# Attention and two wide MLPs on one core: the preparation of the second weights paced anew

## The chip, the cores and the metric

The kernel runs on one core of one Trainium2 chip. The metric is the device time of one execution in microseconds (us), the median of several runs. The engines are named as in the profile: PE is TensorE's matmul, PEld its weight load, DVE is VectorE, ACT is ScalarE, POOL is GpSimd, SP is SyncE, whose queue issues nearly all DMAs here.

## What is computed

An attention whose keys and values are averaged over groups of 8 positions, and two MLPs over its 4608 output rows, all in float32:

```
B, H, S, D = 8, 8, 576, 64          # d_model 512, d_ff 2048
k_p, v_p = mean of k, v over 8 neighbouring positions
attn = softmax(q @ k_p^T / sqrt(D));  x = attn @ v_p       # 4608 x 512
h = x @ w_in;   g = maximum(0.01 * h, h);  x = g @ w_out   # first MLP
h = x @ w_in2;  r = maximum(h, 0);         x = (r * r) @ w_out2   # second MLP
```

The weights of both MLPs come as 64-bit floats and have to be made into 32-bit ones on the chip.

## The kernel before, in words

**Stages.** Attention and the first MLP on 2048 rows run together as four plain tiles of 512 rows (`units`, `first`, `second`). The other 2560 rows of the first MLP and all rows of the second go through nine passes t = 0 to 8 (`HALVES`): passes 0, 1 and 2 are the first MLP (2 x 384, 2 x 384 and 2 x 512 rows, `t < LEAD`), passes 3 to 8 the second MLP (2 x 384 rows each). Every pass has a first half, `first2` (rows times w_in), and a second half, `second2` (times w_out), each of 28 blocks: four slices a = 0 to 3 by seven products 1 to 7 of half matrices, in the manner of Strassen and Winograd. A block takes 12 matmuls in the passes that matter here. The order of products in a second half of passes 0 to 2 is 1, 5, 6, 2, 7, 3, 4, with a running inside.

**What a block needs.** Its weights come over SP's queue into a ring of six buffers (`next_block`, tiles `wb...`, numbered through the program: wb84 to wb111 are the second half of pass 1, wb112 on is pass 2). Products 3, 5, 6 and 7 come as plain float32; ACT rounds them to the upper part (L1118) and DVE subtracts (L1119) to get the lower part. The matmuls are three per product of parts: upper by upper, upper by lower, lower by upper. In a second half the other operand, `oh` (ACT, L1027) and `ol` (DVE, L1028), is made by `split_g` from `g`; there are four buffers of each. Beside that, the second half of pass t makes the operands of pass t + 1: chains of a difference `d` (DVE, L1031), its upper part `xh` (ACT), its lower part `xl` (DVE). Pass 2 has 512 columns, so those chains, made in pass 1's second half, are cut in two and twice as many.

**The preparation of the second weights** (`prepare_products`, L302) has nothing to do with the rows. For each of 8 pairs p and for `in` and `out` it loads two 64-bit slices (`st...`), puts the 32-bit float together (`decode`: ACT L223 absolute value, DVE L225 clamp, L228 shift, L232 join, ACT L241 and DVE L242 low bits), makes four sums (DVE L282 to L286), splits (ACT L324, DVE L325) and stores two results to DRAM. DVE has 10 instructions for an `in` block and 11 for an `out` block, 21 for a pair, 168 in all. The generator yields 7 times for `in` and 8 times for `out`, so a pair is 15 steps and the whole 120, with one more to end it.

**Who calls it.** `prepare_step` (L1363) makes one step. In the last plain tile it is called 2 times for each f below 12 and 3 times after. In the passes it is called after a block (a hook; 56 in a pass, 112 in passes 0 and 1) for three hooks of four, until 105 steps are done, and again from pass 2 on, where the staging pools are opened anew with one buffer instead of two. It has to be over when pass 3 begins.

**What sets the order on an engine.** The program's order is not the order in the queues: a scheduler lists the instructions of every engine by its own estimate of when they are ready, so a step lands earlier or later than the hook at which it is written. On the chip each of DVE and ACT works through its list in order.

Of the kernel before, what the change touches and what calls it, by code (L numbers as in the profile page):

```python
# [32 lines left out]
def attention_two_mlps(  # L33
# [21 lines left out]
    NF = DFF // P  # L55
# [10 lines left out]
    HALVES = (384, 384, 512) + (384,) * 6  # L66
    GROWN = 2
    PADS = {0: 88, GROWN: 88, 3: 48}
    PREP_AHEAD = 105
    LEAD = 3  # L70
    NPASS = len(HALVES) - LEAD
    HMAX = max(HALVES)
# [229 lines left out]
    def prepare_products():  # L302

        for p in range(NQ):
            for kind in ("in", "out"):
                st = fetch_weights(2, [(kind, p), (kind, p + NQ)])
                yield
                ops = ppool.tile([P, 4, HD], F32, tag="ops", name=f"ops_{kind}{p}")
                words = ops.bitcast(U32)
                if kind == "in":  # L310
                    words = words.rearrange("p (i a) x -> p i (a x)", i=2)
                else:
                    words = words.rearrange("p (a i) x -> p i a x", i=2)
                for _ in decode(st, words, f"{kind}2_{p}"):
                    yield
                yield
                s = raw(mpool.tile([P, 2, TT], U32, tag="m", name=f"s2_{kind}{p}"))
                s = s.rearrange("p i (a x) -> p (i a) x", a=2)
                sums(s, *(ops[:, i] for i in range(4)))
                later(1, out=WS[2, kind, p // 2][:, :, p % 2].rearrange("o p x -> p o x"), in_=s)  # L320
                yield
                hl = ppool.tile([P, 3, 2, HD], F32R, tag="hl", name=f"hl2_{kind}{p}")
                for d, i in ((slice(0, 2), slice(0, 2)), (slice(2, 3), slice(3, 4))):
                    nc.scalar.copy(hl[:, d, 0], ops[:, i])  # L324
                    nc.vector.tensor_tensor(out=hl[:, d, 1], in0=ops[:, i], in1=raw(hl[:, d, 0]), op=ALU.subtract)  # L325
                later(
                    3, out=WD[2, kind, p // 2][:, :, p % 2].rearrange("o p x -> p o x"),
                    in_=raw(hl).rearrange("p o h x -> p o (h x)"),
                )
                yield  # L330
# [658 lines left out]
    FIRST2 = []  # L989
# [362 lines left out]
    at_work, due = True, 0  # L1352
    prep, preparing, hooks, prepared = None, True, 0, 0
# [21 lines left out]
    for i, (t, f) in enumerate(units):  # L1375
        if f == NF - 3 and t + 1 < NTILE:
            while ready[0] * S < min((t + 2) * TT, PLAIN):
                advance()
            put_stores(made)
            load_x(t + 1)  # L1380
        if f == NF - 1 and t + 1 < NTILE:
            split_x(t + 1)

        rate = RATES[min(t, 1)]
        if i + 1 < len(units):
            first(*units[i + 1])
        tick()
        if i + 2 < len(units):
            split_weights("in", *units[i + 2])
        if i + 1 < len(units):  # L1390
            split_weights("out", *units[i + 1])
        while at_work and made < due + rate // 2:
            advance()
        second(t, f)
        tick()
        due += rate
        while at_work and made < due:
            advance()
        if w1 < NF:
            prepare_weights(w1)  # L1400
            w1 += 1
        elif t > 0:
            held(lambda: next(sums1, None))
        if i == NF:
            behind(marks[0], 3000)
        if t == NTILE - 1 and f >= NQ - 2 and not at_work:
            if x2pool is None:
                assert not at_work and next(sums1, 1)
                w_early_stack.close()
                x2pool = high_stack.enter_context(tc.tile_pool(name="x2", bufs=1, side="right", reuse_waits="tile"))  # L1410
                dpart = high_stack.enter_context(tc.tile_pool(name="d2", bufs=1, side="right", reuse_waits="tile"))
                ring = high_stack.enter_context(tc.tile_pool(name="ring", bufs=RING, side="right", reuse_waits="tile"))
                load_x2(0)
                tick(9)
                blocks.insert(0, next_block())
            else:
                if xg is None:
                    xg = products_x(0)
                for _ in range(2):
                    next(xg, None)  # L1420
        if x2pool is not None:
            if prep is None:
                ppool = prep_stack.enter_context(tc.tile_pool(name="prep", bufs=1, side="right", reuse_waits="tile"))
                prep = prepare_products()
            for _ in range(2 if f < NF - 4 else 3):
                prepare_step()
    for _ in xg:
        pass
# [14 lines left out]
    for t in range(LEAD + NPASS):  # L1443
# [12 lines left out]
        for half in (first2, second2):  # L1456
            for _ in half(t):
                tick()
                hooks += 1
                if hooks % 4 and (prepared < PREP_AHEAD or t >= GROWN):  # L1460
                    prepare_step()


# [27 lines left out]
```

## Time and profile before

| | us |
|---|---|
| three runs | 1634.41, 1638.08, 1639.64 |
| median | 1638.08 |
| profiled execution, its own time | 1636.4 |
| span of the profiled execution | 1634.7 |
| PE busy in it | 1596.6 |
| DVE busy in it | 1376.9 |
| ACT busy in it | 985.9 |

The passes lie in the span as follows: the last plain tile ends at 526.6 us; pass 0 runs to 645.3 us (halves from 527.6 and 587.4 us), pass 1 to 777.7 us (halves from 645.3 and 707.5 us), pass 2 to 930.3 us (halves from 777.7 and 854.1 us). The bounds are the places where PE's operands turn from `wb_in` to `wb_out` and back. "Busy" of an engine is the union of its instructions' times; the wait in brackets behind an instruction is the engine's idle time before it, with what released it.

### The profile page before, as it was taken

To read this page: it belongs to the slowest core of one execution; us is meant where nothing else is said; L and a number is where in the kernel's file an instruction comes from. 1 tells how busy PE (TensorE), PEld (TensorE's weight loads), DVE (VectorE), ACT (ScalarE), POOL (GpSimd) and SP (SyncE) were. 2 spreads that over 40 slices of the span, in tenths; PEclk is the share of its full clock that TensorE was granted. 3 is DMA by queue.
4 is the path that set the end of the run, shared out by engine and by line. 5 is a ranking of instruction groups with operands and counts; after the bars stand their busy time and mean duration, and the time that the engine had idled before them with its cause. 6 is when DMAs were issued, how large, how long until landed. Compare 5 with 4: busy or idle time off the path is not lost.

```text
span 1634.7 us, 25145 instructions
## 1 busy us (share of the span) xinstructions
PE 1596.6 (98%) x8680; PEld 1433.0 (88%) x8680; DVE 1376.9 (84%) x2049; ACT 985.9 (60%) x1845; POOL 119.3 (7%) x146
## 2 busy tenths in 40 slices
PE   6999999999999999998999999999999999999999
PEld 5877888888887999997888898998998998998997
DVE  6998778788868899899849589789799799799697
ACT  6787677655665776776556447456446455455454
POOL 3202232223210000000000000000000000000000
PEclk9999999999999999999999999999999999999999
DMA  8765536676454997997754664865865766756655
GB/s 217 230 207 152 152 100 189 202 242 211 147 172 149 318 317 262 316 323 223 261 187 124 214 215 147 287 194 150 275 192 170 259 180 195 237 180 204 203 166 176
DMA packets 225327, 340.89 MB, mean 209 GB/s; under 512 B 55728, under 2 KB 138672, under 8 KB 225200
## 3 DMA queue, kind: packets, MB, share of 16 engines
q1 hardware_dynamic: 222048, 337.58, 65.0%
q10 hardware_dynamic: 3152, 1.70, 0.4%
q8 instruction: 69, 1.13, 0.3%
q14 instruction: 58, 0.48, 0.1%
HBM read 268.44 MB, written 69.21 MB: 207 GB/s over the span
## 4 chain that ended last, share of the span: by engine, by line
PE 75%; DVE 13%; DMA 4%; ACT 4%; issue 3%; POOL 1%; SPq 0%; ACTq 0%; DVEq 0%; POOLq 0%
PE psum L1219 14%; PE psum L337 12%; PE psum L336 12%; PE psum L335 12%; PE psum L1220 7%; PE h L335 2%; PE h L337 2%; DVE ol L1028 2%; PE h L336 2%; PE acc L335 2%; PE acc L336 2%; PE acc L337 2%; PE s L611 2%; DMA wb_in<-ws_in 1%; DVE xl L1028 1%
## 5 line engine op out<-in xcount | busy, mean ns | idle before, releaser
L1219 PE MATMUL psum<-wb_out,oh 128*128 128x512 f32 x1008 | 350.6, 392 | 0.0
L335 PE MATMUL psum<-xh,wb_in 128*128 128x384 f32 (+1 forms) x1008 | 343.9, 341 | 4.1 <-DVE g L1199 1.2
L336 PE MATMUL psum<-xl,wb_in 128*128 128x384 f32 (+1 forms) x1008 | 343.2, 341 | 0.0
L337 PE MATMUL psum<-xh,wb_in 128*128 128x384 f32 (+1 forms) x1008 | 342.2, 340 | 0.6 <-DVE wb_in L1119 0.6
L1027 ACT CAST oh<-g 128x768 fp32r<-128x768 f32 (+1 forms) x252 | 216.2, 860 | 177.5 <-PE psum L1219 71.4
L1220 PE MATMUL psum<-wb_out,ol 128*128 128x256 f32 x1008 | 281.0, 280 | 0.0
L1028 DVE TENSOR_TENSOR ol<-g,oh 128x768 fp32r<-128x768 f32 (+1 forms) x252 | 246.7, 982 | 11.8 <-ACT oh L1027 11.0
L1219 PEld LDWEIGHTS psum<-wb_out,oh 128*128 128x128 f32 x1008 | 189.2, 188 | 41.8 <-issue 0.8
L335 PEld LDWEIGHTS psum<-xh,wb_in 128*128 128x128 f32 x1008 | 189.2, 188 | 11.5 <-DVE g L1199 1.9
L337 PEld LDWEIGHTS psum<-xh,wb_in 128*128 128x128 f32 x1008 | 189.1, 188 | 5.2 <-DVE wb_in L1119 0.9
L336 PEld LDWEIGHTS psum<-xl,wb_in 128*128 128x128 f32 x1008 | 189.4, 188 | 4.4
L1220 PEld LDWEIGHTS psum<-wb_out,ol 128*128 128x128 f32 x1008 | 189.3, 188 | 0.2
L1119 DVE TENSOR_TENSOR wb_in<-wb_in 128x512 fp32r<-128x512 f32 x144 | 97.8, 688 | 91.1 <-ACT wb_in L1118 91.0
L1031 DVE TENSOR_TENSOR g<-g,g 128x768 f32<-128x768 f32 (+1 forms) x144 | 140.4, 982 | 2.3 <-ACT g L1140 2.0
L1118 ACT CAST wb_in<-wb_in 128x512 fp32r<-128x512 f32 x144 | 89.0, 620 | 77.9 <-DMA wb_in<-ws_in 71.2
L337 PE MATMUL psum<-oh,wb_out 128*128 128x384 f32 (+1 forms) x336 | 118.7, 357 | 6.0 <-DVE wb_out L1119 6.0
L335 PE MATMUL psum<-oh,wb_out 128*128 128x384 f32 (+1 forms) x336 | 118.0, 354 | 1.9 <-ACT oh L1027 1.9
L336 PE MATMUL psum<-ol,wb_out 128*128 128x384 f32 (+1 forms) x336 | 119.2, 355 | 0.3 <-DVE ol L1028 0.3
L1118 ACT CAST wb_out<-wb_out 128x512 fp32r<-128x512 f32 x144 | 89.2, 619 | 41.7 <-DMA wb_out<-ws_out 41.2
L335 PE MATMUL h<-xh,hl_in 128*128 128x512 f32 x256 | 104.0, 406 | 4.3 <-ACT hl_out L260 2.4
L335 PE MATMUL acc<-gh,hl_out 128*128 128x512 f32 x256 | 103.6, 407 | 0.2
L336 PE MATMUL h<-xl,hl_in 128*128 128x512 f32 x256 | 100.7, 393 | 0.5 <-DVE xl L711 0.5
(171 smaller groups left out, 2976.5 us busy)
## 6 DMA issues: line engine op xcount, KB each, us to landing
wb_in<-wd_in SPq DMA_DIRECT2D x108, 512.0 KB, 3.8
wb_out<-wd_out SPq DMA_DIRECT2D x108, 512.0 KB, 4.3
wb_in<-ws_in SPq DMA_DIRECT2D x144, 256.0 KB, 3.2
wb_out<-ws_out SPq DMA_DIRECT2D x144, 256.0 KB, 2.7
out_dram<-o SPq DMA_DIRECT2D x23, 384.0 KB, 5.1
v<-in_v_dram SPq DMA_DIRECT2D x16, 512.0 KB, 4.6
st_in_out<-in_moe_w_in_dram SPq DMA_DIRECT2D x16, 512.0 KB, 4.0
st_in_out<-in_moe_w_out_dram SPq DMA_DIRECT2D x16, 512.0 KB, 5.0
```

The source lines that it names most:

```text
L335: nc.tensor.matmul(outp, ah, bh, start=first, stop=False, **kw)
L336: nc.tensor.matmul(outp, ah, bl, start=False, stop=False, **kw)
L337: nc.tensor.matmul(outp, al, bh, start=False, stop=last, **kw)
L611: nc.tensor.matmul(sc[:n, 2 * m:2 * m + 2].rearrange("p a x -> p (a x)"), qT[:, 2 * e + m, :n], kT[b % 2][:, 2 * e + m].rearrange("p a x - ...
L1027: nc.scalar.copy(hi, src)
L1028: nc.vector.tensor_tensor(out=lo, in0=src, in1=raw(hi), op=ALU.subtract)
L1031: nc.vector.tensor_tensor(out=out_, in0=a, in1=b, op=ALU.subtract)
L1118: nc.scalar.copy(whole[:, 0], raw(whole[:, 1]))
L1119: nc.vector.tensor_tensor(out=whole[:, 1], in0=raw(whole[:, 1]), in1=raw(whole[:, 0]), op=ALU.subtract)
L1219: nc.tensor.matmul(outp, ah, b, start=first, stop=False, skip_group_check=True)
L1220: nc.tensor.matmul(outp[:, 1], al, b[:, 0], start=False, stop=last, skip_group_check=True)
```

## The change

Three numbers of the pace are changed, and one yield is added. The last plain tile calls 3 steps for every f (30 instead of 24). In passes 0 and 1 the steps done may not exceed 30 + 0.56 for each hook, up to 90 instead of 105. From pass 2 on they may not exceed 90 + 0.75 for each hook. Blocks begun after step 90 have one empty step more behind their loads, so 35 steps are left for pass 2, four of them empty.

```diff
-    PREP_AHEAD = 105
+    PREP_AHEAD = 90
+    PACE = (30, 0.56, 0.75)
@@ prepare_products
                 st = fetch_weights(2, [(kind, p), (kind, p + NQ)])
                 yield
+                if prepared > PREP_AHEAD:
+                    yield
@@ last plain tile
-            for _ in range(2 if f < NF - 4 else 3):
+            for _ in range(3):
                 prepare_step()
@@ passes
                 tick()
                 hooks += 1
-                if hooks % 4 and (prepared < PREP_AHEAD or t >= GROWN):
+                due = PACE[0] + PACE[1] * hooks
+                if t >= GROWN:
+                    due = PREP_AHEAD + PACE[2] * (hooks - 2 * GROWN * len(FIRST2))
+                if prepared < (due if t >= GROWN else min(due, PREP_AHEAD)):
                     prepare_step()
```

No matmul, load or store is added or left out; the 168 DVE instructions of the preparation stay 168. Counted in DVE's queue, cut where the first result of a first half (`g2_t_0_11`) and the last slice's `g2_t_3_12` are read:

| stretch of DVE's queue | preparation before | now |
|---|---|---|
| up to pass 0 | 42 | 43 |
| pass 0, first half | 29 | 28 |
| pass 0, second half | 23 | 22 |
| pass 1, first half | 32 | 31 |
| pass 1, second half | 31 | 12 |
| pass 2, first half | 11 | 32 |

Of the 31 of pass 1's second half, 21 stand in DVE's queue ahead of `o2_1_3`, the last result of that half that DVE reads, and 10 behind it; now 3 ahead and 9 behind.

The first place is DVE's queue in the second half of pass 1, at the weights of product 3 (`wb103` is the last block of product 7, `wb104` the first of product 3). `ol2_1_a_k` is the lower part for slice a and product k, `xl2_2` and `d2_2` are the chains for pass 2, `wm_out2_6` is the preparation of pair 6. Before:

```order
L225 TENSOR_SCALAR wm_out2_6_8327<-wm_out2_6_8327 128x1024
L1031 TENSOR_TENSOR d2_2_7_1_0_8324<-xl2_2_7_8067,xl2_2_1_8015 128x256
L228 TENSOR_SCALAR wm_out2_6_8327<-wm_out2_6_8327 128x1024
L1028 TENSOR_TENSOR xl2_2_5_8210<-d2_2_7_1_0_8324,xh2_2_5_8211 128x256
L1119 TENSOR_TENSOR wb103_out3_7_8329<-wb103_out3_7_8329 128x512
L1031 TENSOR_TENSOR d2_2_7_1_0_8324<-xl2_2_3_8093,d2_2_7_1_0_8324 128x256
L1028 TENSOR_TENSOR ol2_1_1_3_8397<-g2_1_1_22_7502,oh2_1_1_3_8396 128x768
L1028 TENSOR_TENSOR xl2_2_6_8212<-d2_2_7_1_0_8324,xh2_2_6_8213 128x256
L232 SCALAR_TENSOR_TENSOR wm_out2_6_8327<-st2_out6_out14_8296,wm_out2_6_8327 128x1024
L1031 TENSOR_TENSOR d2_2_7_1_0_8324<-xl2_2_2_8043,d2_2_7_1_0_8324 128x256
L1119 TENSOR_TENSOR wb104_out0_3_8358<-wb104_out0_3_8358 128x512
```

Now:

```order
L1034 TENSOR_TENSOR d2_2_7_1_0_8282<-xl2_2_7_8031,xl2_2_1_7983 128x256
L1031 TENSOR_TENSOR ol2_1_3_7_8302<-g2_1_3_12_7762,oh2_1_3_7_8301 128x768
L1031 TENSOR_TENSOR xl2_2_5_8176<-d2_2_7_1_0_8282,xh2_2_5_8177 128x256
L1122 TENSOR_TENSOR wb103_out3_7_8285<-wb103_out3_7_8285 128x512
L1034 TENSOR_TENSOR d2_2_7_1_0_8282<-xl2_2_3_8054,d2_2_7_1_0_8282 128x256
L1031 TENSOR_TENSOR ol2_1_0_3_8330<-g2_1_0_22_7362,oh2_1_0_3_8329 128x768
L1031 TENSOR_TENSOR xl2_2_6_8178<-d2_2_7_1_0_8282,xh2_2_6_8179 128x256
L1122 TENSOR_TENSOR wb104_out0_3_8313<-wb104_out0_3_8313 128x512
```

Pair 6 of the preparation is gone from between the splits, and the splits of `wb103` and `wb104` stand four instructions apart.

The second place is ACT's queue at the end of the same half and the beginning of pass 2 (`oh2_1_a_4` is the last product, `wm_in2_7` the absolute value of pair 7, which needs the loaded `st2_in7`). Before:

```order
L324 CAST hl2_out6_8546<-ops_out6_8326 128x256
L223 ACTIVATE wm_in2_7_8711<-st2_in7_in15_8692 128x1024
L1027 CAST xh2_2_7_8214<-d2_2_3_0_256_8484 128x256
L1027 CAST oh2_1_1_4_8509<-g2_1_1_11_7499 128x768
L1118 CAST wb113_in0_5_8590<-wb113_in0_5_8590 128x512
```

Now:

```order
L1030 CAST oh2_1_1_4_8467<-g2_1_1_11_7478 128x768
L1030 CAST xh2_2_4_8175<-d2_2_7_1_256_8359 128x256
L1030 CAST oh2_1_2_4_8499<-g2_1_2_11_7625 128x768
L1030 CAST xh2_2_7_8180<-d2_2_3_0_0_8391 128x256
L1030 CAST oh2_1_3_4_8518<-g2_1_3_11_7761 128x768
L1121 CAST wb113_in0_5_8543<-wb113_in0_5_8543 128x512
```

No preparation stands among ACT's last operands of the half any more.

The third place is ACT's queue in the middle of that half, where now the only preparation of ACT in it stands (`so5_1` is the copy of product 5's sum, `st2_in6` the load of pair 6). Now:

```order
L1313 COPY so5_1_7925<-psum_6140 128x768
L1030 CAST xh2_2_6_8179<-d2_2_7_0_0_8181 128x256
L1030 CAST oh2_1_0_2_8126<-g2_1_0_21_7361 128x768
L224 ACTIVATE wm_in2_6_8680<-st2_in6_in14_8644 128x1024
L1030 CAST oh2_1_1_2_8149<-g2_1_1_21_7480 128x768
L1030 CAST xh2_2_4_8175<-d2_2_7_0_0_8181 128x256
L242 ACTIVATE ops_in6_8679<-st2_in6_in14_8644 128x1024
L1030 CAST oh2_1_2_2_8167<-g2_1_2_21_7627 128x768
```

Before, the absolute value of pair 6 stood between the operands of product 6 (`oh2_1_0_6` and `oh2_1_1_6`); now it stands between those of product 2. Its two loads stood around the loads of `wb91` and `wb92` in SP's queue, and stand now around that of `wb96`.

## Rows read from the trace of the kernel before

**Rows 1.** The page, busy time of the engines: us (share of the span) xinstructions.

```profile
PE 1596.6 (98%) x8680; PEld 1433.0 (88%) x8680; DVE 1376.9 (84%) x2049; ACT 985.9 (60%) x1845; POOL 119.3 (7%) x146
```

**Rows 2.** Busy time by stretch, from the last plain tile to pass 3.

```profile
core 0: us, PE busy (x) PEld busy (x) DVE busy (x) ACT busy (x) POOL busy (x), PEclk, DMA share, GB/s
472.00:526.60 54.60, 54.19 (x237) 44.00 (x235) 46.09 (x80) 38.19 (x69) 0.00 (x0) 1.00 0.59 204
527.60:587.40 59.80, 58.64 (x337) 58.32 (x338) 50.72 (x75) 40.97 (x59) 0.00 (x0) 1.00 0.93 314
587.40:645.30 57.90, 56.94 (x328) 56.41 (x327) 56.80 (x84) 42.66 (x65) 0.00 (x0) 1.00 0.85 282
645.30:707.50 62.20, 60.84 (x348) 59.93 (x348) 55.11 (x82) 43.69 (x64) 0.00 (x0) 1.00 0.91 310
707.50:777.70 70.20, 62.98 (x342) 60.06 (x341) 67.29 (x109) 47.37 (x76) 0.00 (x0) 0.98 0.81 266
777.70:854.10 76.40, 75.58 (x334) 62.23 (x333) 48.99 (x61) 44.55 (x55) 0.00 (x0) 1.00 0.69 227
854.10:930.30 76.20, 76.20 (x338) 63.12 (x337) 64.98 (x74) 43.22 (x56) 0.00 (x0) 1.00 0.51 154
930.30:988.50 58.20, 58.20 (x336) 57.92 (x335) 45.33 (x55) 28.71 (x40) 0.00 (x0) 1.00 0.70 224
```

**Rows 3.** PE's waits in pass 1's second half: us in total, times, longest.

```profile
PE psum L337 <- DVE wb_out L1119: 5.0, 4, 1.7
PE psum L335 <- ACT oh L1027: 1.9, 1, 1.9
```

**Rows 4.** Busy time and granted clock in the stretch behind these waits.

```profile
768.40:773.00 4.60, 4.60 (x17) 4.21 (x17) 4.60 (x9) 3.23 (x5) 0.00 (x0) 0.63 0.34 114
```

**Rows 5.** DVE's instructions in pass 1's second half: start, us, what [idle before].

```profile
718.10 0.69 DVE L1119 TENSOR_TENSOR wb_out<-wb_out 128x512 fp32r<-128x512 f32 x1
718.70 0.95 DVE L1031 TENSOR_TENSOR g<-g,g 128x768 f32<-128x768 f32 x1
719.57 0.95 DVE L1028 TENSOR_TENSOR ol<-g,oh 128x768 fp32r<-128x768 f32 x1
...
721.91 0.69 DVE L225 TENSOR_SCALAR wm_in<-wm_in 128x1024 f32<-128x1024 f32 x1
722.51 0.69 DVE L1119 TENSOR_TENSOR wb_out<-wb_out 128x512 fp32r<-128x512 f32 x1
...
726.93 1.22 DVE L232 SCALAR_TENSOR_TENSOR wm_in<-st_in_in,wm_in 128x1024 uint32<-128x1024 uint32 x1
728.06 1.82 DVE L1028 TENSOR_TENSOR ol<-g,oh 128x768 fp32r<-128x768 f32 x2
...
732.41 0.42 DVE L282 TENSOR_TENSOR s_in<-ops_in 128x256 f32<-128x256 f32 x1
732.74 0.42 DVE L283 TENSOR_TENSOR s_in<-ops_in 128x256 f32<-128x256 f32 x1
...
737.11 0.42 DVE L1031 TENSOR_TENSOR d<-xl,d 128x256 f32<-128x256 f32 x1
737.45 0.95 DVE L1028 TENSOR_TENSOR ol<-g,oh 128x768 fp32r<-128x768 f32 x1
...
749.13 0.69 DVE L1119 TENSOR_TENSOR wb_out<-wb_out 128x512 fp32r<-128x512 f32 x1
...
761.91 0.68 DVE L1119 TENSOR_TENSOR wb_out<-wb_out 128x512 fp32r<-128x512 f32 x1
...
767.16 0.42 DVE L1028 TENSOR_TENSOR xl<-d,xh 128x256 fp32r<-128x256 f32 x1 [1.16 <-ACT xh L1027]
```

**Rows 6.** ACT's instruction that waits at the end of that half.

```profile
765.72 1.12 ACT L223 ACTIVATE wm_in<-st_in_in 128x1024 f32<-128x1024 f32 x1 [2.58 <-DMA st_in_in<-in_moe_w_in_dram]
```

**Rows 7.** The load of the preparation in that half: KB each, median us to landing.

```profile
st_in_in<-in_moe_w_in_dram SPq DMA_DIRECT2D x4, 512.0 KB, 5.6
```

**Rows 8.** PE's one wait in pass 2's first half.

```profile
784.07 0.50 PE L335 MATMUL psum<-xh,wb_in 128*128 128x512 f32 x1 [0.82 <-ACT s L1189]
```

## The prediction

> **What bounds the kernel now.** The page's first part comes first: PE is busy 1596.6 us of a span of 1634.7 [rows 1], so not more than 38.1 us can be won by anything that leaves the matmuls as they are. Where those lie is read from the busy time by stretch [rows 2]. From the second half of pass 2 on PE is busy all the time (76.20 of 76.20 us, then 58.20 of 58.20): nothing later can take back what an earlier pass gains or loses, and a microsecond saved before 854 us is one off the end. The first half of pass 3 also gives the bare price of a half of 28 blocks at 384 columns: 58.2 us for 336 matmuls, 2.08 us a block. Passes 0 and 1 have four such halves. They take 59.8, 57.9, 62.2 and 70.2 us. The odd one is the second half of pass 1: 70.2 - 58.2 = **12.0 us** too long, and in it DVE is busy 67.29 us, more than the 58.2 that PE needs.
>
> The waits say the same [rows 3]: 5.0 us for DVE's split of a weight block, four times, and 1.9 us for ACT's operand. With the smaller ones PE stands idle 70.20 - 62.98 = 7.2 us [rows 2]. Behind them the granted clock is 0.63 on average for 4.6 us, part of the time at 1.2 instead of 2.4 GHz, [rows 4]: 4.6 x 0.37 = 1.7 us more. The rest of the 12.0 are restarts after a wait and matmuls of the neighbouring halves in the window.
>
> **The price of one preparation, and of the queue.** In pass 1's second half DVE works one instruction behind the other, and there the start of one instruction to the start of the next is what it costs [rows 5]: a split of a weight block 0.60 us (718.10 to 718.70), an instruction on 768 elements 0.87, on 256 of a chain 0.34, L225 0.60, L232 1.13, a sum 0.33. L228 and L325's larger part are like L225, L242 like L232 for `in` and twice 0.61 for `out`. A pair is then 0.60 + 0.60 + 1.13 + 1.14 + 4 x 0.34 + 0.60 + 0.34 = 5.8 us for `in` and as much for `out`, 11.6 us for 21 instructions.
>
> Check on the queue of before, from the split of `wb91` (718.10) to that of `wb107`, the last of product 3: 12 splits, 22 of 768, 24 of 256 and 15 of the preparation (9.3 us) make 7.2 + 19.1 + 8.2 + 9.3 = 43.8 us; the trace has 761.91 - 718.10 = 43.8 [rows 5]. `wb107` is the 24th block of the half; PE, without waits, would take it at 707.4 + 23 x 2.08 = 755.2 and reads the lower part 0.3 us later. DVE is done at 762.6: 7 us late. For `wb103` (749.13 + 0.69 against 707.4 + 19 x 2.08 + 0.3 = 747.2) it was 2.6 us. Lateness grows with each preparation in between.
>
> **The change part by part.**
> (1) *Second half of pass 1.* By the order, 21 preparation instructions ahead of the half's last result become 3, and two of these lie before 718 us; in the stretch I walk there is one (0.6 us). The same walk in the queue of now: to `wb107` 12 splits, 26 of 768, 22 of 256, one of the preparation: 7.2 + 22.6 + 7.5 + 0.6 = 37.9, so it starts at 756.0, ends at 756.7 and is 1.2 us late instead of 7. That is the worst place: to `ol2_1_3_4`, the last operand, it is 42.7 us (13 splits, 28 of 768, 26 of 256, one of 1024, one preparation), done at 761.7 against a need at 763.6; to `wb114`, pass 2's third block, 47.5 us, done at 766.3 against 771. So of the 12.0 us 1.2 remain from DVE alone. The wait for ACT [rows 3] goes too: it comes from the absolute value of pair 7, which stood in ACT's queue 2.58 us for its load [rows 6] with `oh` behind it, and which is no longer there. With the waits the slow clock goes.
> What is late next is the hand-over of the chains: `d` on DVE, `xh` on ACT, `xl` on DVE again. One of them cost DVE 1.16 us [rows 5]; with less in between there will be more of it. Pass 0's second half is the nearest row: DVE busy 56.80 of 57.90, so 1.1 us of such gaps, and PE idle 0.96 [rows 2]. I take 1.0 us on top. Bounds for this half: nothing left (-12.0) to 16 hand-overs of 0.4 us each on top of the 1.2 (-12.0 + 7.6 = -4.4). Taken: -12.0 + 1.2 + 1.0 = **-9.8 us**.
>
> That sum stands on spacings. The Trainium skill, "VectorE: DVE Perf Modes", section "The DRAIN you can't avoid", has each operation followed by a flush of the pipeline during which a next one that is held does not start, so that an instruction costs its duration. The trace does not agree here: instructions of 0.95 us start 0.87 us apart [rows 5]. Priced by durations (0.69, 0.95, 0.42), the walk of now to `wb107` would be 42.9 us instead of 37.9, the block 6.2 us late, the gain 5 us less and the time 1633.7; it lies with rival A, and 0.03 of A's chance is its own.
>
> (2) *First half of pass 2.* The order puts 32 preparation instructions there instead of 11. 21 more at 11.6 us: DVE goes from 48.99 to about 60.6 of 76.4 us, 79% [rows 2]. Cover: the DVE gaps of that half. The halves that carry as many are pass 0's and pass 1's first ones, at 50.72 of 59.8 (85%) and 55.11 of 62.2 (89%), where PE is idle 1.2 and 1.4 us; here it is idle 0.8 already [rows 2, 8]. Bounds -0.8 to +2.2; taken +0.4, since a smaller share of DVE is taken than there.
> (3) *Last plain tile.* Six steps more by the code, one instruction more by the order (42 to 43). PE's idle time there is 0.41 us [rows 2]; bounds -0.4 to +1.0, taken 0.
> (4) *Passes 0 and 1 elsewhere.* The counts are 29 to 28, 23 to 22, 32 to 31: the pace is evened in the code, but hardly in the queue. Idle 1.16, 0.96 and 1.36 us [rows 2]; 0 taken, within 1 us each way.
> (5) *The empty steps, the loads and stores.* The same DMAs move with their blocks; SP's queue carries two pairs of loads later, into a half whose DMA share is 0.69 against 0.81 [rows 2]. 0 taken.
>
> Sum: -9.8 + 0.4 = **-9.4 us**. On the profiled execution's 1636.4 that is 1627.0; the median of the runs lies 1.7 us above it at 1638.08, so I forecast 1638.1 - 9.4 = **1628.7 us**.
>
> **Rivals.**
> *A, most of the gain is held back at ACT (no change within 0.3%).* DVE is no longer short of time, but each link of the 16 chains now follows its ACT cast more closely, and ACT's list is in order, with `oh` of 0.84 us between. At 0.4 us a link, with 1.2 from the split: -4.4 + 0.4 = -4.0, so 1634. For it: the 1.16 us wait [rows 5] arose with more between the links. Against it: ACT is busy only 47.37 of 70.2 us [rows 2], and loses the preparation's share.
> *E, no change, 1638: PE's waits only change their name.* PE has its work for 98% of the span [rows 1], none of which is touched; what DVE no longer holds up, the loads of the weight blocks would, with the DMA engines busy for 0.81 of that half and 0.91 of the one before [rows 2]. Against it: that half's DMA share falls with the loads that leave it, and pass 0's second half runs at 0.85 with PE idle 0.96 us.
> The Trainium skill, "Perfetto Trace Analysis", section "Identifying the Most-Contended Engine", says that improving a kernel generally means improving its most contended engine, which over the whole span is PE; by that the time is E's. The trace disagrees for the one half in which DVE's 67.29 us exceed PE's work [rows 2].
> *B, slower: ACT stands still behind late loads.* The place is the absolute value of pair 6, now between the operands `oh` of product 2, with its loads issued five blocks later in SP's queue than before. A load lands 5.6 us after its issue [rows 7]. The second of them follows that of `wb96`, whose buffer is free after `wb90` (the 7th block), at 707.4 + 7 x 2.08 = 722; it lands near 728. `oh2_1_1_2` behind it is needed at 707.4 + 13 x 2.08 = 734, so there are some 6 us to spare, less the cast and the subtraction. If the load is later than about 732, PE waits, and the three blocks left for pass 2, each with one staging buffer, stop ACT likewise. Price: 5.6 + 1.7 here and 1.9 + 1.7 for each of the three there [rows 3, 4, 7]: +18.1 against -10.8, so +7.3 or 1645.
> *C, more than forecast.* Hand-overs cost nothing, and the waits of passes 0 to 2 shrink as well: -12.0 + 1.2 - 0.8 - 2.5 = -14, so 1624.
> *D, the change does not do what it says.* For passes 0 and 1 nearly so (4); for the place that matters the order shows that it does.
>
> **How the numbers follow.** Forecast (1626 to 1632) 0.60, A 0.20, E 0.04, B 0.06, C 0.08, D 0.02. The range leaves out B, D, E, the far end of A and some of C: **1624 to 1636**. A measurement of this kernel can tell about 0.3%, 4.9 us, from no change. Faster by more than that is below 1633.2: forecast, C and the near part of A (0.05), 0.73. Within 0.3%: the rest of A, D and E, 0.21. Slower: B, 0.06.
>
> **What would show it.** Right: the second half of pass 1 takes about 60 us, PE's wait for the split of `wb_out` falls from 5.0 to near 1 us, its wait for `oh` is gone, the clock stays at 1.00 there, and DVE's share in the first half of pass 2 is near 79% with PE's idle time under 2 us. Wrong: DVE has gaps in that half that ACT's `xh` ends (A); ACT waits for `st_in_in` there (B); or PE waits in the first half of pass 2 for `wb_in` or for a sum that DVE reads late, which (2) has at 0.4 us.

## The result and the profile after

The changed kernel takes 1624.1 us (median of five runs, 1622.5 to 1628.5) against 1638.1 of the kernel before on the same chip (five runs, 1634.4 to 1644.1): ratio 0.9916, with an interval of 0.9889 to 0.9943. Beside the first experiments it took 1623.9 again, ratio 0.9917 (0.9902 to 0.9932). It is faster by 14.0 us by the medians. The profiled executions are 1624.1 and 1636.4 us, 12.3 apart; the missing 1.7 is what the profiled execution of before lay under its own median.

In the changed kernel the code stands one to three lines further down: the split of a weight block (L1119 before) is L1122, ACT's casts (L1027) are L1030, DVE's differences (L1028, L1031) L1031 and L1034. First the page's busy line, which answers to [rows 1]: PE has the same 8680 matmuls, at 1592 instead of 1597 us.

```profile
PE 1592.3 (98%) x8680; PEld 1431.8 (88%) x8680; DVE 1377.1 (85%) x2049; ACT 988.5 (61%) x1845; POOL 118.6 (7%) x146
```

The busy time by stretch, with the same halves as [rows 2]: the last plain tile, the two halves of each of passes 0 to 2, the first half of pass 3.

```profile
473.00:527.60 54.60, 54.11 (x238) 44.13 (x236) 49.05 (x84) 39.07 (x70) 0.00 (x0) 1.00 0.59 205
528.60:587.50 58.90, 58.60 (x336) 58.28 (x337) 47.03 (x71) 40.26 (x57) 0.00 (x0) 1.00 0.94 319
587.50:646.50 59.00, 58.55 (x338) 58.23 (x338) 57.21 (x83) 42.27 (x65) 0.00 (x0) 1.00 0.83 267
646.50:706.30 59.80, 59.00 (x337) 58.06 (x336) 54.63 (x81) 43.39 (x64) 0.00 (x0) 1.00 0.97 330
706.30:765.40 59.10, 58.65 (x339) 58.23 (x338) 58.10 (x93) 42.24 (x67) 0.00 (x0) 1.00 0.77 245
765.40:842.40 77.00, 76.44 (x337) 62.98 (x336) 58.19 (x77) 50.19 (x63) 0.00 (x0) 1.00 0.80 268
842.40:918.60 76.20, 76.20 (x337) 63.09 (x337) 64.99 (x75) 44.01 (x56) 0.00 (x0) 1.00 0.53 170
918.60:976.80 58.20, 58.20 (x336) 57.92 (x335) 45.23 (x55) 28.75 (x40) 0.00 (x0) 1.00 0.70 225
```

The second half of pass 1 fell from 70.2 to 59.1 us: 11.1 of the 12.3 us. Pass 0 and the first half of pass 1 together went from 179.9 to 177.7 (-2.2), but pass 0 starts 1.0 us later (528.6 against 527.6). The first half of pass 2 is 0.6 longer. The remaining 0.6 lies elsewhere. From 842 us on both kernels are alike: PE is busy all the time, as before.

Two of these differences come from something other than the change. In the kernel before, PE runs four matmuls of pass 2 (three from 768.44 us, one at 772.31) ahead of the last block of pass 1, so the 70.2 us hold 342 matmuls [rows 2], where this half holds 334 to 339 in the windows of all other kernels below:

```profile
768.44 0.50 PE L335 MATMUL psum<-xh,wb_in 128*128 128x512 f32 x1
...
772.31 0.63 PE L336 MATMUL psum<-xl,wb_in 128*128 128x512 f32 x1
```

At 76.2 us for 336 such matmuls the four are 0.9 us. On one footing the second half of pass 1 fell from 69.3 to 59.1 us (-10.2), and the first half of pass 2 from 77.3 to 77.0 (-0.3), which fits PE's idle time there: 0.82 us before [rows 2], 0.56 now. The later start of pass 0 is not an effect either: a thousand matmuls earlier, near 330 us and ahead of anything that was changed, this execution is already 1.2 us behind.

PE's waits in pass 1's second half, which answer to [rows 3], are down to one; the clock stays at 1.00 there, and the stretch of [rows 4] has no counterpart.

```profile
PE psum L340 <- DVE wb_out L1122: 0.5, 1, 0.5
```

DVE's row of instructions there, from the split of `wb91` (716.21) to that of `wb107` (754.45), as in [rows 5]: 38.2 us, with no preparation to speak of in between.

```profile
716.21 0.68 DVE L1122 TENSOR_TENSOR wb_out<-wb_out 128x512 fp32r<-128x512 f32 x1
716.82 0.95 DVE L1031 TENSOR_TENSOR ol<-g,oh 128x768 fp32r<-128x768 f32 x1
717.68 0.95 DVE L1034 TENSOR_TENSOR g<-g,g 128x768 f32<-128x768 f32 x1
...
754.45 0.69 DVE L1122 TENSOR_TENSOR wb_out<-wb_out 128x512 fp32r<-128x512 f32 x1
```

### The profile page after: what moved, and what is told of

Its sections match the earlier page's. It is cut to its first block, busy times and chain, and to the rows that moved or that the text cites. A ratio compares the mean times of both kernels' runs of the same rounds, so it can differ in the third digit from the quotient of the medians.

```text
span 1622.4 us, 25133 instructions
## 1 busy us (share of the span) xinstructions
PE 1592.3 (98%) x8680; PEld 1431.8 (88%) x8680; DVE 1377.1 (85%) x2049; ACT 988.5 (61%) x1845; POOL 118.6 (7%) x146
## 4 chain that ended last, share of the span: by engine, by line
PE 76%; DVE 12%; DMA 5%; ACT 4%; issue 2%; POOL 0%; SPq 0%; ACTq 0%; DVEq 0%; POOLq 0%
PE psum L1222 13%; PE psum L338 13%; PE psum L340 13%; PE psum L339 12%; PE psum L1223 7%; PE h L338 2%; PE h L340 2%; PE h L339 2%; PE acc L338 2%; PE acc L339 2%; PE acc L340 2%; DVE ol L1031 2%; PE s L614 1%; ACT x L631 1%; DMA wb_out<-ws_out 1%
## 5 line engine op out<-in xcount | busy, mean ns | idle before, releaser
L1030 ACT CAST oh<-g 128x768 fp32r<-128x768 f32 (+1 forms) x252 | 215.9, 860 | 165.8 <-PE psum L1222 72.1
L1031 DVE TENSOR_TENSOR ol<-g,oh 128x768 fp32r<-128x768 f32 (+1 forms) x252 | 246.4, 981 | 12.5 <-ACT oh L1030 11.8
L1122 DVE TENSOR_TENSOR wb_in<-wb_in 128x512 fp32r<-128x512 f32 x144 | 98.0, 688 | 85.2 <-ACT wb_in L1121 85.1
L1034 DVE TENSOR_TENSOR g<-g,g 128x768 f32<-128x768 f32 (+1 forms) x144 | 140.3, 980 | 0.9 <-ACT g L1143 0.7
```

The costliest lines, as they stand in the source:

```text
L1030: nc.scalar.copy(hi, src)
L1031: nc.vector.tensor_tensor(out=lo, in0=src, in1=raw(hi), op=ALU.subtract)
L1034: nc.vector.tensor_tensor(out=out_, in0=a, in1=b, op=ALU.subtract)
L1122: nc.vector.tensor_tensor(out=whole[:, 1], in0=raw(whole[:, 1]), in1=raw(whole[:, 0]), op=ALU.subtract)
```

## The experiments

Two numbers are read from each kernel's trace. One is the length of pass 1's second half; what it has over 58.2 us, the bare price of 28 blocks [rows 2], is its excess (for the kernel before, 69.3 - 58.2 = 11.1). The other is how late the split of `wb107` is done: its end, less the start of the half, 23 blocks of 2.08 us and 0.3 us (48.1 us in all), the way the prediction reckoned it for the kernel before. The theory T1 says that DVE's queue in this half is what cost the 12 us: whatever stands in it ahead of that split is paid for once DVE's slack is used up. The rivals are the even pace (P), ACT's wait for a load (b), and the DMA traffic.

**The limit alone, on the old pace (e1).**

```
-    PREP_AHEAD = 105
+    PREP_AHEAD = 90
```

> The kernel before with PREP_AHEAD = 90 alone: old steps beside the last plain tile (24), old pace (three hooks of four). By the order passes 0 and 1 carry the same preparation as before up to the last group of pass 1's first half, and pass 1's second half one preparation instruction ahead of its last result instead of 21. T1 (DVE's queue in that half is the whole of it): second half of pass 1 about 59 us instead of 70, total 1638 - 11 = 1627, passes 0 and first half of 1 as before (59.8, 57.9, 62.2 us). Rival P (the even pace does it): second half stays near 68 us or the waits move to pass 1's first half, total 1634 or more. If T1 holds for the half and the even pace has a part of its own, this kernel is about 2 us slower than the changed one, all of it before 708 us.

Measured: 1626.9 us, ratio 0.994 (0.9926 to 0.9953), against 1623.9 and 0.9917 (0.9902 to 0.9932) of the changed kernel beside it. The stretches from pass 0 to pass 1's second half, and PE's one wait in the last of them:

```profile
528.00:588.80 60.80, 58.85 (x336) 58.24 (x337) 50.50 (x75) 40.49 (x59) 0.00 (x0) 1.00 0.91 311
588.80:648.90 60.10, 59.30 (x342) 58.84 (x341) 59.20 (x86) 43.08 (x65) 0.00 (x0) 1.00 0.83 277
648.90:708.70 59.80, 58.40 (x334) 57.44 (x333) 52.67 (x79) 43.24 (x63) 0.00 (x0) 1.00 0.92 313
708.70:767.50 58.80, 58.60 (x338) 58.20 (x337) 57.31 (x91) 41.85 (x67) 0.00 (x0) 1.00 0.74 243
```

```profile
PE psum L337 <- DVE wb_out L1119: 0.2, 1, 0.2
```

The limit alone brings the half to 58.8 us. What the changed kernel has over e1, 2.9 us by the medians, lies ahead of 708 us.

**The even pace, with the old limit (e2).**

```
-    PREP_AHEAD = 90
-    PACE = (30, 0.56, 0.75)
+    PREP_AHEAD = 105
+    PACE = (30, 0.70, 0.75)
```

> The changed kernel with 105 steps done before pass 2 as in the old one, at the even pace (30 beside the last plain tile, 0.70 per block). By the order 21 preparation instructions stand ahead of the last result of pass 1's second half again, spread 12, 3, 6 instead of 10, 4, 7. T1: that half takes 68 to 71 us, PE waits for the split of wb_out by 4 us or more, total 1637. Rival P (the pace): half near 60 us, total near 1626.

Measured: 1638.3 us, ratio 1.0008 (1.0000 to 1.0017). The half and PE's waits in it:

```profile
709.70:777.80 68.10, 61.26 (x337) 57.77 (x336) 66.40 (x108) 46.74 (x75) 0.00 (x0) 1.00 0.81 267
```

```profile
PE psum L340 <- DVE wb_out L1122: 3.5, 4, 1.4
PE psum L338 <- ACT oh L1030: 2.0, 2, 1.1
PE psum L339 <- DVE ol L1031: 1.2, 2, 0.6
```

Spreading the 21 instructions evenly doesn't help while they stay in this half. Rival P falls as a cause of the large part. That the total equals that of the kernel before is partly luck: here the second half of pass 0 is long as well (64.2 us from 586.8 on, with 3.2 us of waits for `wb_out`), since this pace puts 21 preparation instructions into it instead of 11.

**DVE work alone, put back (e4).** On top of e1, multiplications by 1.0 of a dead tile, on DVE only, in the blocks of this half:

```
+                elif t < GROWN and prepared == PREP_AHEAD and hooks % 5:
+                    one = dead[0].rearrange("p a x -> p (a x)")
+                    nc.vector.tensor_scalar(out=one, in0=one, scalar1=1.0, scalar2=None, op0=ALU.mult)
```

> The kernel of e1 with about 19 more DVE instructions in pass 1's second half: a multiplication by 1.0 in place on a dead 128x1024 tile of the preparation, 0.60 to 0.69 us each, 11 to 13 us in all, on DVE alone: no load, no store, nothing on ACT. T1 (it is DVE's time in the queue): the half is back at 68 to 73 us, PE waits for wb_out again, total 1636 to 1641. Rivals: if ACT's casts of the preparation, or ACT's 2.58 us wait for the load, or the DMA traffic made the old loss, the half stays at 60 us and the total at 1627 as in e1.

Measured: 1629.7 us, ratio 0.996 (0.9946 to 0.9974). That is 2.8 us over e1 where 9 to 14 were expected. The half, the added instructions in it, and PE's waits for DVE:

```profile
709.10:771.70 62.60, 60.07 (x337) 57.87 (x336) 62.46 (x102) 41.74 (x66) 0.00 (x0) 1.00 0.72 230
```

```profile
L1467 DVE TENSOR_SCALAR ops_out<-ops_out 128x1024 f32<-128x1024 f32 x15 | 10.3, 686 | 0.0
```

```profile
PE psum L339 <- DVE ol L1031: 0.8, 2, 0.5
PE psum L340 <- DVE wb_out L1122: 0.8, 2, 0.5
```

The dose was smaller than written. Only 12 of the added instructions start ahead of the split of `wb107`; at 0.60 us they are 7.2 us, and in the order three instructions on 768 elements (2.6 us) went behind that split to make room. With e1's slack (58.80 - 57.31 = 1.5 us of DVE) some 3 us are left, and the split is done 3.4 us late (759.94 + 0.68 - 709.1 - 48.1), in e1 0.5. The result fitted T1 in size only after this count, so the dose was raised, with the lateness written down first.

**The same with more of it (e8).**

```
+                elif t < GROWN and prepared == PREP_AHEAD:
+                    one = dead[0].rearrange("p a x -> p (a x)")
+                    for _ in range(1 + (hooks % 4 == 0)):
+                        nc.vector.tensor_scalar(out=one, in0=one, scalar1=1.0, scalar2=None, op0=ALU.mult)
```

> The kernel of e4 with more of the same DVE-only instructions: one per block of pass 1's second half and a second one at every fourth. Counted in DVE's order, 17 stand between the splits of wb91 and wb107 (in e4 8, in the kernel before 15 of the preparation). T1, worked out by the walk that the prediction used: from wb91 to wb107 37.3 + 17 x 0.60 = 47.5 us; wb91 starts some 9.5 us after the half's first matmul, so wb107 is done 9.5 + 47.5 + 0.7 = 57.7 us after it against a need at 48.1: 9.6 us late. e4 by the same walk was 3.4 us late, and its half 3.8 us longer than e1's. So the half is 9 to 11 us longer than e1's 58.8, and the total 1636 to 1638. If DVE's time is only part of what the kernel before lost (ACT's wait for a load, ACT's casts, DMA traffic being the rest), the half stays below 64 us and the total below 1632, as e4's 1629.7 could also be read.

Measured: 1638.2 us, ratio 1.0003 (0.9991 to 1.0015). The half is 70.2 us, against 69.3 of the kernel before, with ACT at 41.14 instead of 47.37 us and the DMA share at 0.66 instead of 0.81 [rows 2]. Below it four microseconds behind its waits, where the granted clock is 0.58, as in [rows 4]; from 754 to 758 us it is 0.57 as well, behind the longest wait.

```profile
712.00:782.20 70.20, 63.76 (x335) 60.69 (x334) 68.28 (x110) 41.14 (x66) 0.00 (x0) 0.95 0.66 204
...
768.00:772.00 4.00, 4.00 (x16) 4.00 (x16) 4.00 (x9) 0.69 (x2) 0.00 (x0) 0.58 0.39 97
```

```profile
PE psum L340 <- DVE wb_out L1122: 3.9, 6, 2.2
PE psum L338 <- issue: 1.6, 1, 1.6
PE psum L338 <- ACT oh L1030: 0.5, 1, 0.5
PE psum L339 <- DVE ol L1031: 0.4, 1, 0.4
```

`wb107` is done 10.3 us late (769.73 + 0.68 - 712.0 - 48.1), where 9.6 was written; `wb91` began 2.9 us later and the stretch behind it was 2.2 us shorter than reckoned. An edit that adds DVE instructions alone, no load and no work of ACT, brings back as much as the kernel before lost. It does so at a larger lateness (10.3 us against 7), and one part of it comes by way of ACT: behind `wb107` ACT waits for the loads of pass 2's weight blocks, with `xh` and `oh` next in its list, and DVE waits 1.62 us for that `xh`:

```profile
776.53 0.62 ACT L1121 CAST wb_in<-wb_in 128x512 fp32r<-128x512 f32 x1 [2.17 <-DMA wb_in<-ws_in]
```

**Half the dose of the real thing (e3).** The kernel before with `PREP_AHEAD = 97`:

```
-    PREP_AHEAD = 105
+    PREP_AHEAD = 97
```

> The kernel before with PREP_AHEAD = 97: half of pair 6 stays in pass 1's second half, the block `in`, with 10 DVE instructions, its load and its ACT work, all between the splits of wb91 and wb107; the block `out` goes to pass 2. T1: 37.3 + 5.8 = 43.1 us from wb91 to wb107, 4 to 5.6 us late by the walk, half 63 to 64.5 us, total 1631 to 1632.5. If the loss came from the last load or from pair 7 at the end of the half, this kernel is as fast as e1 (1627) or as slow as before (1636), not between.

Measured: 1631.9 us, ratio 0.9966 (0.9954 to 0.9979), between e1 and the kernel before. The half is 62.0 us, somewhat under what was expected, and `wb107` 3.0 us late (762.66 + 0.68 - 712.2 - 48.1).

```profile
712.20:774.20 62.00, 59.41 (x334) 57.37 (x333) 58.01 (x92) 42.69 (x68) 0.00 (x0) 1.00 0.84 265
```

**ACT's wait for the load of pair 7 taken away (e9).** The kernel before, with ACT's instructions of pair 7 ordered behind the half's last result, so that no `oh` stands behind them:

```
+        if t == GROWN:
+            last_act = [i for i in nc.cur_bb.bb.instructions if i.engine == mybir.EngineType.Activation][-1]
...
                     prepare_step()
+                    if t == GROWN:
+                        for ins in traced[begin:]:
+                            if ins.engine == mybir.EngineType.Activation:
+                                tc.add_manual_dep(
+                                    ins, last_act.name,
+                                    mybir.DependencyInfo(mybir.DependencyClass.NoSync, mybir.DependencyReason.DATA),
+                                    reason="held",
+                                )
```

> The kernel before, with ACT's instructions of pair 7 kept behind the last result of pass 1's second half in ACT's order; DVE's order in that half is unchanged, with its 21 preparation instructions. This takes away the 2.58 us in which ACT waited for a load with the operands oh behind it. Rival (b), ACT's wait for the load makes a good part of the loss: PE's wait for oh (1.9 us) and part of the slow clock go, total 1632 to 1634. T1: DVE's queue is what is late, so the same instants are only waited for under another name; half 69 to 70 us, total 1636 to 1638.

Measured: 1636.3 us against 1637.9, ratio 0.9989 (0.9977 to 1.0001). The half and PE's waits in it (this execution, at 1642.4 us, was the slowest of eleven; it was 3 us behind before pass 0 and 8 us when the half began, in parts that the edit doesn't touch):

```profile
715.60:784.40 68.80, 61.53 (x336) 57.48 (x336) 66.31 (x108) 44.74 (x73) 0.00 (x0) 1.00 0.83 274
```

```profile
PE psum L337 <- DVE wb_out L1119: 5.0, 4, 1.7
PE psum L335 <- ACT oh L1027: 1.1, 2, 0.7
PE psum L336 <- DVE ol L1028: 1.1, 3, 0.5
```

The wait for `wb_out` is the same 5.0 us in four pieces as in [rows 3], and `wb107` is 7.4 us late (770.40 + 0.68 - 715.6 - 48.1), as in the kernel before. The wait for `oh` falls from 1.9 to 1.1, and the clock is 1.00 instead of 0.98 in this half, which is 68.8 us against 69.3. By the medians the load of pair 7 costs 1.6 us, with an interval that includes zero. It is not the bulk. The test of rival (b) is not a clean one, though: at the same place ACT now waits for a weight block of pass 2, again with `xh` and `oh` behind it.

```profile
776.41 0.62 ACT L1118 CAST wb_in<-wb_in 128x512 fp32r<-128x512 f32 x1 [2.02 <-DMA wb_in<-ws_in]
```

**ACT work alone (e6).** On top of e1, copies of the dead tile on ACT at every other block:

```
+                elif t < GROWN and prepared == PREP_AHEAD and hooks % 2:
+                    one = dead[0].rearrange("p a x -> p (a x)")
+                    nc.scalar.copy(one, one)
```

> The kernel of e1 with 12 more ACT instructions in pass 1's second half (a copy in place of a dead 128x1024 tile, 1.12 us each by the nearest row, 13 us in all, 7 of them before the last product), on ACT alone: nothing on DVE, no load. In the kernel before ACT had some 5.5 us more in that half than in e1. T1 (only DVE's queue counts there): ACT has 17 us of idle time in that half (41.85 busy of 58.8), so the half grows by 0 to 2 us, total 1627 to 1629. Rival (b), the preparation's share of ACT with oh and xh queued behind it made the loss: half 64 us or more, total 1632 or more.

Measured: 1626.1 us, ratio 0.9937 (0.9923 to 0.9951), as fast as e1. Ten of the copies lie in the half:

```profile
709.50:769.30 59.80, 58.74 (x338) 58.30 (x337) 57.45 (x91) 50.12 (x78) 0.00 (x0) 1.00 0.76 241
```

```profile
L1467 ACT COPY ops_out<-ops_out 128x1024 f32<-128x1024 f32 x10 | 10.5, 1050 | 0.0
```

10.5 us of ACT cost 1.0 us in the half; 10.3 us of DVE in e4 cost 3.8, and 16.4 us in e8 (24 of them, each 0.685 us) cost 11.4.

The kernels side by side, in us. The lateness of `wb107` is worked out as above (that of the kernel before stands in the prediction); the third column does the same for the half's last `ol`, whose need lies 27 blocks and 0.2 us behind the start (56.4 us). A minus means that it was early. The totals come from several chips, on which the kernel before took 1636.2 to 1638.1.

| kernel | `wb107` late | last `ol` late | half | excess over 58.2 | total (median) |
|---|---|---|---|---|---|
| e1 | 0.5 | -2.7 | 58.8 | 0.6 | 1626.9 |
| changed | 0.7 | -2.5 | 59.1 | 0.9 | 1624.1 |
| e3 | 3.0 | 3.7 | 62.0 | 3.8 | 1631.9 |
| e4 | 3.4 | 5.2 | 62.6 | 4.4 | 1629.7 |
| before | 7 | 11.8 | 69.3 | 11.1 | 1638.1 |
| e9 | 7.4 | 11.5 | 68.8 | 10.6 | 1636.3 |
| e2 | 9.2 | 9.5 | 68.1 | 9.9 | 1638.3 |
| e8 | 10.3 | 12.9 | 70.2 | 12.0 | 1638.2 |

Where `wb107` is late by 3 us or more, the excess lies 0.7 to 1.7 us above its lateness, but for two kernels: e9 has 3.2 and the kernel before 4.1. In these two, six preparation instructions stand between that split and the last `ol` (in e2 two, in e4 and e8 two of the added ones, in e3 none), some 2.3 us of DVE's time at the prediction's prices that the lateness of `wb107` leaves out. Counted at the last `ol`, every late kernel's excess is within 1 us of its lateness. For the kernel before it ends at 775.70 us:

```profile
774.75 0.95 DVE L1028 TENSOR_TENSOR ol<-g,oh 128x768 fp32r<-128x768 f32 x1
```

So the bulk of the loss is DVE's queue. ACT's waits for loads (1.2 us of DVE's idle time in the kernel before, 1.6 in e8) and the slow clock are mixed into the rest; these runs don't take them apart, and the DMA traffic was never added by itself.

**What the changed kernel has over e1 (again, e10).** The changed kernel ran a second time, beside e1:

> The changed kernel once more, beside e1 on the same chip. T1: 1624, the second half of pass 1 at 59 us. What it has over e1 is the price of the even pace and of the six steps more beside the last plain tile: by the traces of before and after -2 us before 706 us, of which the start of pass 0 is +1.0.

Measured: 1623.9 us, with the start of pass 0 at 529.7. That start varies from one execution to the next: it lies between 527.8 and 529.7 us in the kernels with 30 steps beside the last plain tile and between 527.6 and 530.8 in those with 24. So the +1.0 us that the expectation names does not come from the change. Then the old pace with the new 30 steps:

```
-    PACE = (30, 0.56, 0.75)
+    PACE = (30, 0.75, 0.75)
```

> The changed kernel with the old pace of three blocks in four in passes 0 and 1 (0.75 instead of 0.56), the 30 steps beside the last plain tile kept, and 90 steps as the limit. It tells apart what the changed kernel has over e1 (2.9 us): the even pace, or the six steps beside the last plain tile. If the even pace: about 1626.5, with pass 0's first halves 60 to 61 us and the waits for the chain's g, s and wb again. If the six steps: about 1624.

Measured: 1630.1 us, ratio 0.9952 (0.9939 to 0.9964), slower than both cases foresaw. The loss is not in pass 0's first half (59.2 us) but in its second, and under the same name:

```profile
588.70:654.30 65.60, 61.28 (x338) 59.14 (x337) 64.45 (x95) 45.26 (x68) 0.00 (x0) 0.97 0.88 294
```

```profile
PE psum L340 <- DVE wb_out L1122: 4.3, 5, 1.9
```

In this stretch DVE starts 23 preparation instructions, in that of the changed kernel 11. So the even pace is worth something: it keeps pass 0's second half under the same limit. Without it the 30 steps would have cost 6.6 us (65.6 against 59.0), with a slow stretch of the clock in it (0.97).

The smaller part shows in the first half of pass 1. With the old pace PE waits there for `s` and for the split of `wb_in`, here in e3; the seven kernels with that pace (before, e1, e3, e4, e6, e8, e9) show 1.3 to 4.6 us of such waits, all with one for `wb_in`. Those with the even pace or with 30 steps (changed, twice, e2, e7, e10, e11, e12) show 0 to 1.4 us, none for `wb_in`.

```profile
PE psum L335 <- ACT s L1193: 2.2, 1, 2.2
PE psum L337 <- DVE wb_in L1119: 0.9, 1, 0.9
```

From the start of pass 0 to that of pass 1's second half those seven take 179.4 to 184.8 us; the five that have the even pace and at most 90 steps (changed, twice, e7, e11, e12) take 176.4 to 178.1. The kernel before, at 179.9, lies near the lower end of its group, so the 2.2 us between the two profiles are rather too few.

**More moved to pass 2 (e7, e11, e12).** e7 leaves one more pair for pass 2, e11 half a pair, e12 is e7 with the old 24 steps:

```
-    PREP_AHEAD = 90
-    PACE = (30, 0.56, 0.75)
+    PREP_AHEAD = 75
+    PACE = (30, 0.42, 1.0)
...
-                if prepared > PREP_AHEAD:
-                    yield
```

> The changed kernel with one more pair moved to pass 2: 75 steps before it (pace 0.42 per block), one step per block in pass 2. By the order pass 0 and the first half of pass 1 carry 21 preparation instructions less, the first half of pass 2 the same 41, and its second half 21 instead of 0. That half has DVE busy 65.0 of 76.1 us; 21 more at 11.6 us make 76.6 of 76.1. T1, read by the stage: that half becomes bound by DVE and ends 1 to 5 us later, pass 0 and pass 1 give at most the 1.5 us back that PE still waits there, total 1624 to 1628. Rival (any work taken out of passes 0 and 1 is won): 1622.

Measured: 1623.8 us, ratio 0.9935 (0.9917 to 0.9953): not to be told from the changed kernel. The second half of pass 2 was to become bound by DVE. DVE is indeed full there, and PE doesn't wait at all, so the expectation's way of reading the stage failed here:

```profile
840.10:916.40 76.30, 76.30 (x339) 63.22 (x338) 75.44 (x96) 49.84 (x66) 0.00 (x0) 1.00 0.66 224
```

e11 (`PREP_AHEAD = 82`, `PACE = (30, 0.48, 0.85)`):

> Between the changed kernel and e7: 82 steps before pass 2 (0.48 per block), so that pass 2's second half carries 11 preparation instructions: DVE 65.0 + 5.8 = 70.8 of 76.1 us. T1: room enough there, and up to 1.5 us of PE's waits in passes 0 and 1 to win: 1622 to 1624, hardly to be told from the changed kernel.

Measured: 1627.9 us, ratio 0.9946 (0.9929 to 0.9963), 4 us over its expectation. Its profiled execution (1624.8) shows no cause for it: DVE busy 70.31 of 76.2 us in pass 2's second half, no wait of PE there. Its five runs lie between 1624.7 and 1631.3. This miss stays open.

e12 (e7 with the old rule for the last plain tile and `PACE = (24, 0.47, 1.0)`):

> The kernel of e7 (75 steps before pass 2) with the old 24 steps beside the last plain tile and 0.47 steps per block after it. In e7 and in the changed kernel PE's first wait in pass 0 is 1.4 us for ACT's cast of the preparation's hl_out; with 24 steps it should be 1.0 us for o and 0.2 for gl, as in the kernel before. If the 30 steps matter only by this wait, e12 is 0 to 0.5 us faster than e7: 1623 to 1624. If the 30 steps, by taking work out of pass 0, save the 1.2 us wait for g and more in pass 0's first half, e12 is 1 to 2.5 us slower than e7: 1625 to 1626.

Measured: 1626.6 us, ratio 0.9941 (0.9923 to 0.9958), an interval that overlaps e7's almost wholly. PE's waits at the start of pass 0 are again those of the kernel before (1.0 us for `o` and 0.2 for `gl` instead of 1.4 for `hl_out`), and pass 0's first half takes 59.9 us instead of 59.1. The size of the six steps beside the last plain tile is below what these runs can tell. No kernel here beats the changed one by more than the measurement is uncertain.

## Why the prediction was right

The forecast was 1628.7 us and the time is 1624.1: the sign and the place were right, and 4.6 us more were won. Of these, 1.7 are the difference between the medians and the profiled executions; the other 2.9 by the steps. The step that was missed by most is (4), which was taken at nothing.

(1) *Second half of pass 1.* Forecast -9.8, measured -11.1 as the prediction cut the half, -10.2 without the four matmuls of pass 2; the 12.0 us that it started from were 11.1. The walk through DVE's queue gave 37.9 us from `wb91` to `wb107`; the trace has 38.2. The split of `wb107` was put at 1.2 us late and is 0.7; PE waits 0.5 for it. The term that failed is the +1.0 for the hand-overs of the chains: DVE waits in this half only

```profile
DVE wb_out L1122 <- ACT wb_out L1121: 0.6, 2, 0.3
DVE g L1034 <- ACT g L1143: 0.2, 1, 0.2
```

and never for `xh`. It is ACT that waits for DVE's `d`:

```profile
ACT xh L1030 <- DVE d L1034: 10.0, 13, 1.4
```

DVE stays the slower partner of each chain even when it has less to do, busy 58.10 of 59.1 us. The 1.16 us wait for `xh` in [rows 5] was read as a sign of what would come; it was a consequence of ACT's own delay behind the load [rows 6]. (Such a wait can come back without that load: e8 has one of 1.62 us.)

That the walk counted starts, not durations, held. The Trainium skill, "VectorE: DVE Perf Modes", section "The DRAIN you can't avoid", lets the next operation start only when the pipeline is empty, but adds that one that is not held starts earlier. The trace fits the second: instructions of 0.95 us start 0.87 us apart. So the prediction's "does not agree" holds only against the first. By durations the stretch would have been 42.9 us and the time 1633.7; measured were 38.2 and 1624.1.

(2) *First half of pass 2.* Forecast +0.4, measured +0.6 by the windows, -0.3 with the four matmuls put back where they belong: PE's idle time fell from 0.82 to 0.56 us. The sign was wrong, and the size too small to matter. DVE is busy 58.19 of 77.0 us, 76%, where 79% was forecast.

(3) *Last plain tile.* Taken at 0, and 0 within 0.2 us. PE's first matmul of pass 0 now waits for ACT's cast of the preparation, 1.37 us where it waited 1.03 us for `o` before; in return a wait of 0.23 us for `gl` is gone. The 1.0 us by which pass 0 starts later was there before the tile began.

```profile
528.59 0.41 PE L338 MATMUL psum<-xh,wb_in 128*128 128x384 f32 x1 [1.37 <-ACT hl_out L327]
```

(4) *Passes 0 and 1 elsewhere.* Taken at 0 within 1 us for each of three halves, measured -2.2 in all, and between the two groups of kernels above rather more. "The pace is evened in the code, but hardly in the queue" was read from counts by half (28 instead of 29, 22 instead of 23, 31 instead of 32). Counts don't show where in a half an instruction stands, and with the pace the waits for `s` and `wb_in` in the first half of pass 1 went. e10 shows the other side: twelve more in pass 0's second half cost 6.6 us. Which moved instruction took which wait away was not tested.

(5) *Loads and stores.* Nothing shows.

The sum of the parts by the windows is -11.1 - 2.2 + 1.0 (start of pass 0) + 0.6 - 0.6 (elsewhere) = -12.3; the +1.0, the -0.6 and the 1.7 between profile and median were forecast by no step, and they lie where the two kernels hardly differ.

The rivals: A needed DVE to wait for ACT, and the waits run the other way. E took PE, busy for 98% of the span, for the only bound; e8 speaks against it, since DVE work alone in one half of 59 us moves the half by 11 us and the total as much (e8 against e1). The Trainium skill, "Perfetto Trace Analysis", section "Optimization Strategy", says that the most contended engine may change between the regimes of a kernel; this trace agrees, with DVE at 67.29 us against PE's 62.98 in that one half [rows 2]. B needed a load that ACT meets some 4 us too early; ACT waits for `st_in_in` once in pass 1's second half and once in the first half of pass 2, and PE in neither case:

```profile
ACT wm_in L224 <- DMA st_in_in<-in_moe_w_in_dram: 1.0, 1, 1.0
...
ACT ops_in L242 <- DMA st_in_in<-in_moe_w_in_dram: 1.4, 1, 1.4
```

C (1624) had the number: its hand-overs that cost nothing and the smaller waits in passes 0 and 1 came true, the smaller wait in pass 2 by 0.3 of its 0.8 us.

## What to carry to other kernels

Read each stage's own bound, and walk the queue of the engine that is late there, instruction by instruction from start to start: the walk through the changed queue was within 0.3 us of 38.2. It has to be a walk through the queue as it will be: in e3 and e8 the added work was put on top of another kernel's queue, and the stretch came out 3.6 and 2.2 us shorter than that (39.5 and 45.3 us). Set against the instant at which the consumer needs the last result of the stage, the lateness is close to what the stage loses. When filler work is spread, count it against that lateness half by half; it is nearly free up to the slack (22 instructions in pass 0's second half, 3 in pass 1's) and costs time beyond (3.8 us for 10.3 us of DVE in e4, 11.4 for 16.4 in e8). An edit that adds such instructions alone, on dead data, is a cheap way to price a queue.

## What the runs showed that was not expected

- DVE can be full and cost nothing. In e7 it is busy 75.44 of 76.30 us in pass 2's second half and PE never waits there, while in e3, with 58.01 of 62.0 us, it is what PE waits for. The share says only that little is left; whether a result is late depends on what stands ahead of it in the queue.
- Copies of 10.5 us on ACT cost 1.0 us of time in e6 (ACT busy 50.12 instead of 41.85 us), with its in-order list holding the operands `oh` and `xh`.
- The slow clock came back by DVE work alone: in e8 the granted clock is 0.58 for 4 us, part of the time at 1.2 instead of 2.4 GHz, behind 4 us in which PE was busy for 2.07 us. The same happened 14 us earlier (0.57 from 754 to 758 us, behind 4 us with 1.84 us of PE). In such a stretch the clock loses 1.7 us (4.0 x 0.42), a part of the price of a late queue:

```profile
764.00:768.00 4.00, 2.07 (x10) 1.46 (x10) 4.00 (x8) 0.81 (x2) 0.00 (x0) 0.99 0.67 244
```
